# Expert stage: plain fp32 matmuls in two 64-column tiles in place of split weights

## The chip, the cores and the metric

The kernel runs on one core of a Trainium2 chip. The metric is the time of the program on the device in microseconds (us), the median of several runs. Engines are named as the profile names them: PE is TensorE's matmul and PEld its weight load, DVE is VectorE, ACT is ScalarE, POOL is GpSimd, SP is SyncE, which only issues DMAs here.

## The reference

Three layers follow each other: attention over pooled queries, a dense layer of the form `(h - tanh(h)) @ w_out`, and a routed mixture of experts. Only the last is touched:

```python
N, D, E, F = 1152, 512, 8, 1024          # tokens, model, experts, hidden
cap = N // E * 2                          # 288 rows for each expert
expert = argmax(x @ w_gate)               # one expert for each token
gate = softmax(x @ w_gate)[expert]
# tokens go to their expert in order, up to cap; later ones are dropped
h = maximum(disp[e] @ w1[e], 0)           # (cap, 512) @ (512, 1024)
y = h @ w2[e]                             # (cap, 1024) @ (1024, 512)
out[i] = gate[i] * y[expert[i], pos[i]]   # dropped tokens stay zero
```

All inputs and outputs are float32.

## The kernel before

Every step of work is an operation with candidate engines, costs and a due time (`at`). A planner, `Plan.run`, goes through them when the program is built: it takes the operation that can start earliest, finds it a place in SBUF or PSUM, and emits its instructions. Between operations marked `seq`, those of the expert stage, each engine keeps the order of their due times. DMA issues on SP are such a lane too.

The expert stage is `moe2`. Routing has sorted the tokens into a DRAM array `xs`, 288 rows for each expert, by indirect DMAs (`scatter`, L1102). The first 64 rows of each expert are handled by code that always runs; the rows 64 to 287, the overflow, by code inside `tc.If(count > 64)`, on PE, DVE and POOL. The tokens of the first two experts come from one-hot matmuls (L1181); those of the other six are loaded from `xs` (L1158) and transposed on PE (L1190). They stand in four tiles `xT`, two experts in each.

PE multiplies fp32 data in the rounded type fp32r, which keeps fewer bits. To keep accuracy each number is split: a rounded part, and what it leaves. A chunk of weights is 128 partitions x 1024 numbers, 8 for each expert (4 of `w1`, 4 of `w2`), 64 in all. `chunk` loads it by SP (L1224), copies it to the rounded type (L1235, through L421 on ACT or L423 on POOL), and subtracts (L1237, through L431 on DVE or L432 on POOL). The token tile `xT` holds the rounded part of 64 tokens and the rest side by side, 128 columns, so one matmul of 512 columns multiplies both with one part of the weights. ACT and DVE then add the two halves of the result, 64 partitions each.

For each expert `hidden` runs twice, once for each half of the 1024 hidden units (eight matmuls, L1249; the sum of halves, L1255 and L1258; four transposes, L1264; ReLU and split, L1268 and L1271), and `project` twice (eight matmuls, L1285). `output` scales by the gate, adds the halves (L1292, L1295) and scatters to the result. For an expert with overflow, `overflow_x`, `_t`, `_e`, `_h`, `_r`, `_y`, `_z` and `_s` fetch, transpose, split, multiply (L1379), apply ReLU, multiply (L1404), scale and scatter up to 224 more rows, with three products for each (rounded by rounded, and two with a rest).

The first 21 chunks (`ntot`) are requested ahead of the stage. Each later one waits until an overflow step of an earlier expert has released its place.

Of the kernel before, what the change touches and what calls it, by code (L numbers as in the profile page):

```python
# [389 lines left out]
class Kernel:  # L390
# [716 lines left out]
    def moe2(self):  # L1107
        nc, tc, P = self.nc, self.tc, self.P
        V = P.v
# [4 lines left out]
        DK, FK = DM // 128, FF // 128  # L1114
        SM = 64
        M = (cap - SM) // 2
        NP_ = 256
# [15 lines left out]
        xT = [P.sb([2, DK, 2, SM], F32R, f"xT{j}") for j in range(E // 2)]  # L1133
# [8 lines left out]
        ho = static([FK // 2, 2, 2, 2 * M], F32R, "ho")  # L1142
        xo = [static([DK, NP_], F32R, f"xo{i}") for i in range(2)]
        xbs = [static([2, 514], F32, f"xb{i}") for i in range(2)]
        yo = [static([512], F32, f"yo{i}") for i in range(2)]
        hs = P.sb([2, 512], F32, "hs")
        hT = P.sb([FK, 2 * SM], F32R, "hT")
        hp, ht, yp, ov = P.ps(2, None, "hp"), P.ps(1, None, "ht"), P.ps(1, None, "yp"), P.ps(4, None, "ov", top=True)
# [4 lines left out]
        def xe():  # L1153
            return P.raw(ho, F32).rearrange("p a b c d -> p (a b c d)")[:, 0:E // 2 * DM].rearrange("p (j d) -> p j d", d=DM)
# [9 lines left out]
        def pads():  # L1164
            for x in xo:
                nc.gpsimd.memset(V(x)[:, :, 2 * M:NP_].bitcast(F32), 0.0)

        P.op([("pool", 0.3, pads)], w=[(x, "pad") for x in xo], at=T2 - 6, name="pads")
        P.op([("dma", 2.2, lambda: ldx(1, E // 2))], r=[self.xs_tok], w=[(ho, 1)], at=T2 - 3.9, name="ldx1")
        P.op([("dma", 0.8, ldg)], r=[self.xs_tok], w=[xg], at=T2 - 3.8, name="ldg")  # L1170
        if CFG["warm"]:
            def warm():
                for i in range(CFG["warm"]):
                    nc.tensor.matmul(out=V(hp)[:, i % 2, 0:256], lhsT=self.ident_r, rhs=self.qz[0].rearrange("p a b c -> p (a b c)")[:, 0:256], start=True, stop=True)

            P.op([("pe", 0.109 * CFG["warm"], warm)], w=[hp], at=T2 - 0.6, name="warm")
# [10 lines left out]
        for j in range(E // 2):  # L1187
# [14 lines left out]
            P.op([("act", a_ps(512), lambda j=j, xpv=xpv: nc.scalar.activation(  # L1202
                out=V(xT[j])[:, :, :, 0, :], in_=xpv(), func=ACTF.Copy))], r=src, w=[(xT[j], 0)], at=at + 0.02,
                name=f"xth{j}")
            P.op([("dve", d1(512), lambda j=j, xpv=xpv: nc.vector.tensor_tensor(  # L1205
                out=V(xT[j])[:, :, :, 1, :], in0=xpv(), in1=V(xT[j])[:, :, :, 0, :].bitcast(F32), op=ALU.subtract))],
                r=src + [(xT[j], 0)], w=[(xT[j], 1)], at=at + 0.04, name=f"xtl{j}")

        def htv(half):
            return V(ht)[:, 0, half * 256:(half + 1) * 256].rearrange("p (f m) -> p f m", m=SM)  # L1210
# [3 lines left out]
        def chunk(e, q, use):  # L1214
            n = used[0]
            used[0] += 1
            wh, wl = w[e, q] = [P.sb([1024], F32R, f"{nm}{e}.{q}") for nm in ("wh", "wl")]

            def ld():
                if q < 4:  # L1220
                    src = w1[e, q % 2 * 256:(q % 2 + 1) * 256, q // 2 * 512:(q // 2 + 1) * 512]
                else:
                    src = w2[e, (q - 4) * 256:(q - 3) * 256]
                nc.sync.dma_start(out=P.raw(wl, F32).rearrange("p (k f) -> p k f", f=512),  # L1224
                                  in_=src.rearrange("(k p) f -> p k f", p=128))
# [13 lines left out]

        def hidden(e, half, at):  # L1240
            for i in range(2):
                q = 2 * half + i
                chunk(e, q, at + 0.87 * i)

                def mm(i=i, q=q):
                    for j in range(2):
                        k = 2 * i + j
                        for wl in range(2):
                            nc.tensor.matmul(out=V(hp)[:, half, :], lhsT=V(xT[e // 2])[:, e % 2, k].rearrange("p a m -> p (a m)"),  # L1249
                                             rhs=V(w[e, q][wl])[:, j * 512:j * 512 + 512],  # L1250
                                             start=(k == 0 and wl == 0), stop=(k == DK - 1 and wl == 1))

                P.op([("pe", 4 * 0.216, mm)], r=[xT[e // 2], *w[e, q]], w=[(hp, half)], at=at + 0.87 * i, name=f"h{e}.{q}")
            D = CFG["hdl"]
            P.op([("act", a_ps(512), lambda: nc.scalar.activation(  # L1255
                out=V(hs)[0:SM, half], in_=V(hp)[SM:2 * SM, half, :], func=ACTF.Copy))], r=[(hp, half)], w=[(hs, half)],
                at=at + D[0], name=f"hsc{e}.{half}")
            P.op([("dve", d1(512), lambda: nc.vector.tensor_tensor(  # L1258
                out=V(hs)[0:SM, half], in0=V(hp)[0:SM, half, :], in1=V(hs)[0:SM, half], op=ALU.add))],
                r=[(hp, half)], w=[(hs, half)], at=at + D[1], name=f"hsa{e}.{half}")  # L1260

            def trh():
                for f in range(4 * half, 4 * half + 4):
                    nc.tensor.transpose(out=V(ht)[:, 0, f * SM:(f + 1) * SM],  # L1264
                                        in_=V(hs)[0:SM, half, (f % 4) * 128:(f % 4 + 1) * 128], identity=ident[0:SM, 0:SM])
# [10 lines left out]
        def project(e, half, at):
            for i in range(2):
                f4 = 2 * half + i
                chunk(e, 4 + f4, at + 0.87 * i)
# [210 lines left out]
```

## Time and profile before

| what | value |
| --- | --- |
| median of 3 runs | 775.77 us (774.8 to 777.73) |
| the profiled execution, first to last instruction | 775.6 us |
| mean granted clock of TensorE | 0.899 of full |
| PE, DVE, ACT, POOL busy | 614.2, 626.6, 438.1, 497.8 us |
| first expert matmul / last | starts at 606.8 us / ends at 770.1 us |

The profile is of one execution and its span is within 0.2 us of the median. Busy times are of whole engines over the whole span; the expert stage is its last fifth. Matmuls are pipelined: one lasts longer than the distance between the starts of two.

### The profile page before, as it was taken

How to read it: one execution, taken by the hardware profiler on the slowest of the kernel's cores; microseconds unless marked ns; L12 is line 12 of the kernel's file. 1: busy time of each engine (PE TensorE's matmuls, PEld its weight loads, DVE VectorE, ACT ScalarE, POOL GpSimd, SP SyncE). 2: the span in 40 equal slices, each digit the busy share in tenths (PEclk: the TensorE clock that was granted, in tenths of full speed). 3: DMA queues.
4: the chain of work that ended last, by engine and by line, in shares of the span. 5: the costliest groups of instructions: out<-in, count | busy, mean ns of one | idle time of the engine just before them, and what ended most of it. 6: DMA issues, size and time to landing. Idle time of an engine off the chain costs nothing. (4 is left out here: it accounts for less than half of the span.)

```text
span 775.6 us, 9909 instructions
## 1 busy us (share of the span) xinstructions
PE 614.2 (79%) x3246; PEld 512.4 (66%) x3246; DVE 626.6 (81%) x784; ACT 438.1 (56%) x698; POOL 497.8 (64%) x359
## 2 busy tenths in 40 slices
PE   4779778788687878676877588799998698569965
PEld 3667666676576667465766477699788585449743
DVE  4998796988889989999999999774846355887483
ACT  5866766676767656655645655566633234452452
POOL 6866575785766766768669676865565516563572
PEclk9989999899999989799799897899967799779997
DMA  9899999999999997903034013233300336666520
GB/s 294 158 190 198 203 195 217 231 211 202 209 219 199 225 203 257 351 3 109 1 122 150 27 29 108 82 98 141 128 28 32 69 109 194 219 223 226 191 103 8
DMA packets 213548, 119.45 MB, mean 154 GB/s; under 512 B 172814, under 2 KB 182030, under 8 KB 213488
## 3 DMA queue, kind: packets, MB, share of 16 engines
q1 hardware_dynamic: 211600, 114.49, 60.3%
q0 software_dynamic: 1680, 3.81, 1.6%
q8 instruction: 33, 0.54, 0.3%
q10 hardware_dynamic: 208, 0.39, 0.2%
q14 instruction: 27, 0.22, 0.1%
HBM read 66.22 MB, written 11.43 MB: 100 GB/s over the span
## 5 line engine op out<-in xcount | busy, mean ns | idle before, releaser
L432 POOL TENSOR_TENSOR b<-b,b 128x512 fp32r<-128x512 f32 (+3 forms) x102 | 197.3, 1941 | 63.3 <-ACT b L421 58.3
L641 POOL TENSOR_SCALAR b<-b 128x1152 f16<-128x1152 int16 (+1 forms) x114 | 138.8, 1233 | 69.7 <-ACT b L633 37.6
L906 PE MATMUL psum<-b,b 128*128 128x512 f32 x432 | 137.4, 443 | 48.2 <-POOL b L432 26.1
L906 PEld LDWEIGHTS psum<-b,b 128*128 128x128 f32 x432 | 88.2, 212 | 71.3 <-POOL b L432 33.7
L421 ACT ACTIVATE b<-b 128x1024 fp32r<-128x1024 f32 (+3 forms) x112 | 95.1, 876 | 71.2 <-DVE b L817 21.2
L842 PE MATMUL psum<-b,b 128*128 128x384 f32 x576 | 125.5, 358 | 1.0 <-ACT b L633 0.7
L842 PEld LDWEIGHTS psum<-b,b 128*128 128x128 f32 x576 | 112.2, 204 | 9.4 <-ACT b L633 1.0
L421 ACT ACTIVATE b<-psum 64x288 f32<-64x288 f32 (+5 forms) x162 | 81.5, 508 | 61.0 <-PE psum L906 14.5
L626 DVE CUSTOM_DVE_ANT_1 b<-psum,na 128x1152 f16<-128x1152 f32 x72 | 97.2, 1350 | 16.5 <-PE psum L620 14.8
L633 ACT ACTIVATE b<-psum,b 128x1152 int32<-128x1152 f32 x72 | 87.8, 1219 | 28.1 <-DVE b L626 16.1
L431 DVE TENSOR_TENSOR b<-b,b 128x1024 fp32r<-128x1024 f32 (+1 forms) x50 | 88.5, 1774 | 16.2 <-ACT b L421 13.6
L620 PE MATMUL psum<-b,b 128*128 128x384 f32 x384 | 89.7, 373 | 14.1 <-ACT b L633 14.0
L661 PE MATMUL psum<-b,b 128*128 128x288 f16 x576 | 88.3, 300 | 4.7 <-DVE b L676 2.8
L423 POOL TENSOR_SCALAR b<-b 128x512 fp32r<-128x512 f32 (+3 forms) x48 | 52.6, 1098 | 53.2 <-DVE b L817 30.6
L620 PEld LDWEIGHTS psum<-b,b 128*128 128x128 f32 x384 | 69.8, 203 | 19.8 <-ACT b L633 19.4
L661 PEld LDWEIGHTS <-b 128*128 128x128 f16 x576 | 54.2, 102 | 24.6 <-issue 11.1
L887 POOL TENSOR_TENSOR b<-b,b 128x768 f32<-128x768 f32 x24 | 52.0, 2168 | 16.9 <-ACT b L876 15.8
L1249 PE MATMUL psum<-b,b 128*128 128x512 f32 x128 | 42.6, 487 | 7.6 <-DVE b L1205 5.9
L495 PE MATMUL psum<-ident_r,b 128*128 128x128 f32 x144 | 22.3, 274 | 21.9 <-DVE b L431 8.4
L1249 PEld LDWEIGHTS psum<-b,b 128*128 128x128 f32 x128 | 29.4, 240 | 15.2 <-DVE b L1205 6.1
L1255 ACT ACTIVATE b<-psum 64x512 f32<-64x512 f32 x16 | 9.5, 594 | 51.4 <-PE psum L1249 32.4
L817 DVE SCALAR_TENSOR_TENSOR b<-b,b 128x512 uint32<-128x512 uint32 x32 | 37.7, 1177 | 1.1
(138 smaller groups left out, 1038.4 us busy)
## 6 DMA issues: line engine op xcount, KB each, us to landing
b<-in_moe_w_dram SPq DMA_DIRECT2D x64, 512.0 KB, 5.5
b<-in_moe_w_in_dram SPq DMA_DIRECT2D x32, 256.0 KB, 4.2
b<-in_moe_w_out_dram SPq DMA_DIRECT2D x16, 512.0 KB, 5.8
xs<-b SPq DMA_DIRECT2D x6, 771.0 KB, 8.9
b<-in_k_dram SPq DMA_DIRECT2D x8, 576.0 KB, 5.3
b<-in_q_dram SPq DMA_DIRECT2D x8, 576.0 KB, 5.7
b<-in_v_dram SPq DMA_DIRECT2D x8, 576.0 KB, 4.9
out_dram<-b SPq DMA_DIRECT2D x3, 768.0 KB, 6.2
```

Of the source, the lines that this page charges most:

```text
L421: "a": ("act", (a_ps if ps else a_sb)(n), lambda: nc.scalar.activation(out=dst(), in_=src(), func=ACTF.Copy)),
L423: "p": ("pool", p1(n), lambda: nc.gpsimd.tensor_scalar(out=dst(), in0=src(), scalar1=1.0, scalar2=0.0, op0=ALU.mult, op1=ALU.add)),
L431: "v": ("dve", d1(n), lambda: nc.vector.tensor_tensor(out=dst(), in0=a(), in1=b(), op=ALU.subtract)),
L432: "p": ("pool", p2(n), lambda: nc.gpsimd.tensor_tensor(out=dst(), in0=a(), in1=b(), op=ALU.subtract)),
L620: nc.tensor.matmul(out=V(S_)[:, j, 0:CB], lhsT=lhsT, rhs=rhs[:, j * CB:(j + 1) * CB], start=(m == 0), stop=(m == len(mm) - 1))
L626: P.op([("dve", 1.27, lambda: nc.vector.tensor_tensor_reduce(out=V(junk), in0=V(S_)[:, :, 0:CB], in1=self.na[:, 3:4].unsqueeze(2).to_broad ...
L633: P.op([("act", 1.2, lambda: nc.scalar.activation(out=V(p).rearrange("p (a e) -> p a e", a=3), in_=V(S_)[:, :, 0:CB], func=ACTF.Exp, bias= ...
L641: P.op([("pool", p1(S), lambda a=a, src=src, by=by: nc.gpsimd.tensor_scalar(out=V(hl)[:, a], in0=src(), scalar1=by, scalar2=0.0, op0=ALU.m ...
L661: nc.tensor.matmul(out=V(ps)[:, 0, 0:half], lhsT=V(v16[n])[:, j].rearrange("p a d -> p (a d)"), rhs=V(pt)[:, hl * KT + j, i * SQ + g * hal ...
L842: nc.tensor.matmul(out=V(h)[:, a, 0:384], lhsT=w, rhs=V(xx)[:, dk, sl], start=(n == 0), stop=(n == 11))
L906: nc.tensor.matmul(out=V(ps)[:, 0, :], lhsT=V(g[gi, blk, i][gl])[:, a, sl], rhs=V(wo[2 * gi + i, a])[:, wl, :], start=(i == 0 and a == 0 a ...
L1249: nc.tensor.matmul(out=V(hp)[:, half, :], lhsT=V(xT[e // 2])[:, e % 2, k].rearrange("p a m -> p (a m)"), rhs=V(w[e, q][wl])[:, j * 512:j * ...
```

## The change

The rounded type leaves the expert stage. Tokens, hidden units and weights stay plain fp32 and are used as they were loaded. The 64 tokens of an expert are the stationary operand, 64 columns. Two matmuls with the same tokens and different weights write the partitions 0 to 63 and 64 to 127 of one PSUM bank, two tiles side by side. In the first layer the two tiles are the halves of the hidden units, in the second the halves of the sum over hidden units; the output adds those two, as it added the two parts before. The ReLU is done on the sums ahead of four full transposes, with one copy after. The first layer of the next expert comes ahead of the transposes of this one. 40 chunks are requested ahead and not 21. Overflow rows use plain fp32 as well: one product in place of three, on 224 columns without padding. `xT` and other buffers get fixed places.

```diff
-        xT = [P.sb([2, DK, 2, SM], F32R, f"xT{j}") for j in range(E // 2)]
+        xT = [static([2, DK, SM], F32, f"xT{j}") for j in range(E // 2)]
+        hs = [static([FH], F32, f"hs{i}") for i in range(2)]
+        hT = [static([FC, 2, SM], F32, f"hT{i}") for i in range(2)]
...
-            at = T2 - 0.5 + (0.0 if j == 0 else 3.2 + 0.2 * j)
+            at = T2 - 0.5 + (0.0 if j == 0 else 4.3 + 0.2 * j)
...
         def chunk(e, q, use):
...
-            wh, wl = w[e, q] = [P.sb([1024], F32R, f"{nm}{e}.{q}") for nm in ("wh", "wl")]
+            c = w[e, q] = P.sb([1024], F32, f"w{e}.{q}")
...
+                if q < DK:
+                    nc.sync.dma_start(out=V(c), in_=w1[e, q * 128:(q + 1) * 128, :])
...
-            P.op(self.copy_alts(lambda: V(wh), lambda: P.raw(wl, F32), 1024, CFG["ehe"][n % 8]),
-                 r=[wl, (ovt, gh)] + (latep if CFG["ehe"][n % 8] == "p" else late), w=[wh], at=at, name=f"ehi{e}.{q}")
-            P.op(self.sub_alts(lambda: V(wl), lambda: P.raw(wl, F32), lambda: V(wh).bitcast(F32), 1024, CFG["ele"][n % 8]),
...
+        def hidden(e, at):
+            h = hp[e % 2]
+            for k in range(DK):
+                chunk(e, k, at + 0.87 * k)
+
+                def mm(k=k):
+                    for i in range(2):
+                        nc.tensor.matmul(out=V(h)[i * SM:(i + 1) * SM, 0, :], lhsT=V(xT[e // 2])[:, e % 2, k],
+                                         rhs=V(w[e, k])[:, i * FH:(i + 1) * FH], start=(k == 0), stop=(k == DK - 1))
+
+                P.op([("pe", 0.87, mm)], r=[xT[e // 2], w[e, k]], w=[h], at=at + 0.87 * k, name=f"h{e}.{k}")
+            P.op([("act", a_ps(512), lambda: nc.scalar.activation(out=V(hs[e % 2]), in_=V(h)[:, 0, :], func=ACTF.Relu))],
+                 r=[h], w=[hs[e % 2]], at=at + 3.6, name=f"hs{e}")
+
+        def turn(e, at):
+            def tr():
+                for c in range(FC):
+                    nc.tensor.transpose(out=V(ht)[:, 0, c * 128:(c + 1) * 128], in_=V(hs[e % 2])[:, c * 128:(c + 1) * 128],
+                                        identity=ident)
+
+            P.op([("pe", FC * 0.11, tr)], r=[hs[e % 2]], w=[ht], at=at, name=f"ht{e}")
+            P.op([("dve", d1(512), lambda: nc.vector.tensor_copy(
+                out=V(hT[e % 2]).rearrange("p c i m -> p (c i m)"), in_=V(ht)[:, 0, :]))],
+                r=[ht], w=[hT[e % 2]], at=at + 0.1, name=f"hT{e}")
+
+        def project(e, at):
+            for c in range(FC):
+                chunk(e, DK + c, at + 0.87 * c)
+
+                def mmy(c=c):
+                    for i in range(2):
+                        nc.tensor.matmul(out=V(yp)[i * SM:(i + 1) * SM, 0, :], lhsT=V(hT[e % 2])[:, c, i],
+                                         rhs=V(w[e, DK + c])[:, i * DM:(i + 1) * DM], start=(c == 0), stop=(c == FC - 1))
...
+        for e in range(-1, E):
+            at = T2 + EP * (e + 1)
+            x0 = xbs[e % 2]
+            n = e + 1
...
+            if e >= 0:
+                over_on("t", "pe", e, at, [x0], [(ov, 0), (ov, 1)])
+                over_on("e", "dve", e, at + 0.6, [(ov, 0), (ov, 1)], [xo])
+            if n < E:
+                hidden(n, at + 0.7)
+            if e >= 0:
+                turn(e, at + 4.4)
+                over(e, 0, at + 5.0)
+                over_on("r", "dve", e, at + 5.2, [ov], [ho])
+                project(e, at + 5.6)
+                output(e, at + 9.2)
+                over(e, 1, at + 9.3)
+                over_on("z", "dve", e, at + 9.5, [(ov, 2), (ov, 3)], [x0])
+                over_on("s", "pool", e, at + 9.6, [x0, self.out_tok], [])
...
     def overflow_h(...):
-                for wl, x in ((0, xh), (0, xl), (1, xh)):
-                    for k in range(DK):
...
+                o = f % 2 * 256
+                for k in range(DK):
+                    nc.tensor.matmul(out=ps[:, f // 2, o:o + 2 * M], rhs=x[:, k, :],
+                                     lhsT=V(wsl[k])[:, f * 128:(f + 1) * 128], start=(k == 0), stop=(k == DK - 1))
     def overflow_y(...):
-                    for a, wl in ((0, 0), (0, 1), (1, 0)):
...
+                    i, c = divmod(f, FC)
+                    nc.tensor.matmul(out=ps[0:M, 2 + j, :], lhsT=V(ho)[:, f, j * M:(j + 1) * M],
+                                     rhs=V(wsl[c])[:, i * DM:(i + 1) * DM], start=(f == 0), stop=(f == FK - 1))
...
-           ... nh=16, ntot=21, ...
+           ... ntot=40, ...
```

Here `SM` is 64, `DK` 4, `FC` 4, `FH` and `DM` 512, `M` 112, `FK` 8. The second layer's loads (not shown) bring rows of both halves of `w2` into one chunk.

## Rows read from the trace of the kernel before

**Rows 1.** The page's table of engines: busy us, share, instructions.
```profile
PE 614.2 (79%) x3246; PEld 512.4 (66%) x3246; DVE 626.6 (81%) x784; ACT 438.1 (56%) x698; POOL 497.8 (64%) x359
```
**Rows 2.** Windows: length, busy PE, PEld, DVE, ACT, POOL, PE clock, DMA share, GB/s.
```profile
620.10:632.00 11.90, 11.90 (x99) 11.84 (x98) 4.83 (x9) 1.44 (x2) 0.00 (x0) 1.00 0.00 1
...
662.00:679.00 17.00, 11.53 (x44) 7.97 (x44) 14.58 (x11) 9.45 (x13) 10.51 (x5) 0.80 0.75 250
...
606.70:775.60 168.90, 133.69 (x636) 103.55 (x636) 108.17 (x104) 66.60 (x88) 80.96 (x42) 0.87 0.47 153
```
**Rows 3.** Groups by form, 600 to 776 us: busy us, mean ns, idle before.
```profile
L431 DVE TENSOR_TENSOR b<-b,b 128x1024 fp32r<-128x1024 f32 x34 | 70.2, 2067 | 4.5 <-ACT b L421 2.0 <-DVEq L1412 1.1 <-DVEq L1387 1.1
L432 POOL TENSOR_TENSOR b<-b,b 128x1024 fp32r<-128x1024 f32 x22 | 59.2, 2698 | 40.3 <-ACT b L421 39.3 <-issue 0.2
L421 ACT ACTIVATE b<-b 128x1024 fp32r<-128x1024 f32 x45 | 45.5, 1049 | 11.1 <-PE psum L1404 6.0 <-PE psum L1379 4.9
...
L1379 PEld LDWEIGHTS psum<-b,b 128*128 128x128 f32 x192 | 23.2, 192 | 0.2
...
L1205 DVE TENSOR_TENSOR b<-psum,b 128x512 fp32r<-128x512 f32 x4 | 2.8, 691 | 6.5 <-ACT b L1202 6.4
```
**Rows 4.** Timelines of one ordinary expert, DVE and PE: start, us, what, idle before.
```profile
735.07 2.08 PE L1249 MATMUL psum<-b,b 128*128 128x512 f32 x8
...
737.86 3.08 DVE L431 TENSOR_TENSOR b<-b,b 128x1024 fp32r<-128x1024 f32 x1
...
741.18 3.04 DVE L431 TENSOR_TENSOR b<-b,b 128x1024 fp32r<-128x1024 f32 x1 [0.24 <-DVEq L1387]
744.14 0.67 DVE L1258 TENSOR_TENSOR b<-psum,b 64x512 f32<-64x512 f32 x1
...
744.87 0.69 PE L1264 MATMUL psum<-ident,b 64*128 64x64 f32 x4 [4.76 <-DVE b L1258]
745.70 3.28 PE L1249 MATMUL psum<-b,b 128*128 128x512 f32 x8
749.28 2.08 PE L1285 MATMUL psum<-b,b 128*128 128x512 f32 x8 [0.30 <-PEq L1350]
```
**Rows 5.** Timeline of SP's queue, 430 to 640 us: its loads of expert weights.
```profile
451.53 106.54 SPq L1224 DMA_DIRECT2D b<-in_moe_w_dram  x21
...
631.31 1.92 SPq L1224 DMA_DIRECT2D b<-in_moe_w_dram  x4
```
**Rows 6.** Timeline of PE, 578 to 650 us.
```profile
595.01 5.85 PE L1181 MATMUL psum<-b,b 128*128 128x128 f32 x50
...
611.55 2.82 PE L1190 MATMUL psum<-ident,b 128*128 128x128 f32 x12 [0.98 <-DMA b<-xs]
...
620.12 11.88 PE L1379 MATMUL psum<-b,b 128*128 128x256 f32 x96
...
635.97 11.40 PE L1404 MATMUL psum<-b,b 128*112 128x512 f32 x48
```
**Rows 7.** Timelines of DVE, POOL, SP's queue and ACT, 578 to 612 us.
```profile
581.87 2.03 DVE L1071 TENSOR_TENSOR b<-b,b 128x24 f32<-128x24 f32 x1
583.93 0.18 DVE L1072 TENSOR_TENSOR b<-b,b 128x24 f32<-128x24 f32 x1
...
596.68 4.61 DVE L431 TENSOR_TENSOR b<-b,b 128x1024 fp32r<-128x1024 f32 x4
...
597.72 4.43 POOL L1102 DMA_INDIRECT xs<-b,xi  x1 [0.30 <-issue]
602.46 0.97 POOL L1102 DMA_INDIRECT xs<-b,xi  x1 [0.30 <-issue]
...
604.75 0.69 SPq L1158 DMA_DIRECT2D b<-xs  x1
...
605.41 0.60 ACT L1202 ACTIVATE b<-psum 128x512 fp32r<-128x512 f32 x1 [9.11 <-DMA xs<-b,xi]
```
**Rows 8.** Timeline of PE: the last matmuls.
```profile
767.95 2.12 PE L1285 MATMUL psum<-b,b 128*128 128x512 f32 x8 [0.93 <-DVEq L1387]
```

More of the change, by code (lines that the diff above doesn't have):

```diff
@@ L1114, in moe2 @@
         DK, FK = DM // 128, FF // 128
+        FH = FF // 2
+        FC = FK // 2
         SM = 64
         M = (cap - SM) // 2
-        NP_ = 256
         T2 = self.t2 + CFG["t2"]
@@ L1141, in moe2 @@
         xg = P.sb([E, 2], F32, "xg")
-        ho = static([FK // 2, 2, 2, 2 * M], F32R, "ho")
-        xo = [static([DK, NP_], F32R, f"xo{i}") for i in range(2)]
+        ho = static([FK, 256], F32, "ho")
+        xo = static([DK, 2 * M], F32, "xo")
         xbs = [static([2, 514], F32, f"xb{i}") for i in range(2)]
[L1145 to L1148, printed above, removed]
+        xT = [static([2, DK, SM], F32, f"xT{j}") for j in range(E // 2)]
+        hs = [static([FH], F32, f"hs{i}") for i in range(2)]
+        hT = [static([FC, 2, SM], F32, f"hT{i}") for i in range(2)]
+        yo = [P.sb([512], F32, f"yo{i}") for i in range(2)]
+        for y in yo:
+            y.limit = P.limit
+        hp = [P.ps(1, None, f"hp{i}") for i in range(2)]
+        ht, yp, ov = P.ps(1, None, "ht"), P.ps(1, None, "yp"), P.ps(4, None, "ov", top=True)
         xv = xs.rearrange("(e s) d -> s e d", s=cap)
@@ L1201, in moe2 @@
                 P.op([("pe", DK * 0.11, trx)], r=[(ho, 1)], w=[(ov, j)], at=at, name=f"xtr{j}")
[L1202 to L1210, printed above, removed]
+            eng = "av"[j % 2]
+            P.op(self.copy_alts(lambda j=j: V(xT[j]), xpv, 512, eng, True), r=src, w=[xT[j]], at=at + 0.02, name=f"xth{j}")
         rel, w, used = {}, {}, [0]
@@ L1240, in hidden @@
[L1240 to L1265, printed above, removed]
-            P.op([("pe", 4 * 0.11, trh)], r=[(hs, half)], w=[(ht, half)], at=at + D[2], name=f"htr{e}.{half}")
-            P.op([("act", a_ps(256), lambda: nc.scalar.activation(
-                out=V(hT)[:, 4 * half:4 * half + 4, 0:SM], in_=htv(half), func=ACTF.Relu))],
-                r=[(ht, half)], w=[(hT, half)], at=at + D[3], name=f"hth{e}.{half}")
-            P.op([("dve", d1(256), lambda: nc.vector.scalar_tensor_tensor(
-                out=V(hT)[:, 4 * half:4 * half + 4, SM:2 * SM], in0=htv(half), scalar=0.0,
-                in1=V(hT)[:, 4 * half:4 * half + 4, 0:SM].bitcast(F32), op0=ALU.max, op1=ALU.subtract))],
-                r=[(ht, half)], w=[(hT, half)], at=at + D[4], name=f"htl{e}.{half}")
@@ L1276, in project @@
[L1276 to L1279, printed above, removed]
-                def mmy(f4=f4):
-                    for f in range(2 * f4, 2 * f4 + 2):
-                        for wl in range(2):
-                            o = (f % 2) * DM
-                            nc.tensor.matmul(out=V(yp)[:, 0, :], lhsT=V(hT)[:, f, :], rhs=V(w[e, 4 + f4][wl])[:, o:o + DM],
-                                             start=(f == 0 and wl == 0), stop=(f == FK - 1 and wl == 1))
-                P.op([("pe", 4 * 0.216, mmy)], r=[(hT, half), *w[e, 4 + f4]], w=[yp], at=at + 0.87 * i, name=f"y{e}.{f4}")
+                if q < DK:
+                    nc.sync.dma_start(out=V(c), in_=w1[e, q * 128:(q + 1) * 128, :])
+                else:
+                    nc.sync.dma_start(out=V(c).rearrange("p (i f) -> p i f", i=2),
+                                      in_=w2[e].rearrange("(i c p) d -> c p i d", i=2, p=128)[q - DK])
@@ L1398, in overflow_y @@
         FK = FF // 128
+        FC = FK // 2
         ps = V(ps4)
@@ L1402, in overflow_y, with overflow_z @@
                 for f in range(FK):
[L1403 to L1408 removed]
+                    i, c = divmod(f, FC)
+                    nc.tensor.matmul(out=ps[0:M, 2 + j, :], lhsT=V(ho)[:, f, j * M:(j + 1) * M],
+                                     rhs=V(wsl[c])[:, i * DM:(i + 1) * DM], start=(f == 0), stop=(f == FK - 1))
+    def overflow_z(self, reg, xb, xo, ho, ps4, SM, M):
         nc, tc, V = self.nc, self.tc, self.P.v
```

118 lines of the change are left out of this document (32 added, 86 removed).

## The prediction

> **What bounds the kernel now.** I read the page's table of engines first. It names no bound: TensorE is busy for 79% of the span, VectorE for 81% [rows 1]. Those are averages over stages, so next come the windows of the stage that the change touches, from the first matmul of the experts (606.7 us) to the end: 168.9 us, in which PE is busy for 133.7, DVE for 108.2 and POOL for 81.0, at a granted clock of 0.87 [rows 2]. Two kinds of stretch hide in that sum. While an overflowing expert runs its extra matmuls (620.1 to 632), PE has no gap and the clock is 1.00. From 662 to 679 us, one ordinary expert, PE is busy for 11.5 of 17.0 us, DVE for 14.6, and the clock is 0.80. Only two of the eight experts overflow; so six are bound by something that is not PE.
>
> The groups of instructions of the stage say what: splitting the weights. L431 takes 70.2 us of DVE, L432 59.2 of POOL, L421 45.5 of ACT [rows 3]. The timeline of one ordinary expert shows how that reaches PE [rows 4]: two subtractions of 3.08 and 3.04 us stand on DVE ahead of the addition L1258, and the transposes L1264 wait 4.76 us for it. The price is paid twice: behind the gap eight matmuls take 3.28 us where eight took 2.08 ahead of it, and with a mean granted clock of 0.80 part of such an expert ran at 1.2 and not at 2.4 GHz.
>
> Loading doesn't limit the stage: 21 chunks were requested by 558 us, and the queue then requested none until 631 us, for want of buffers [rows 5].
>
> **The splits go.** 64 copies and 64 subtractions leave ACT, DVE and POOL, 175 us of the stage in the three groups above. What an ordinary expert leaves to DVE is a copy of 128x512 from PSUM (0.69 us, priced as L1205 [rows 3]) and the multiply-add of the output; to POOL, the scatter. So the gaps of 4.8 us and the slow clock behind them go, and what is late next is PE itself.
>
> **The price of plain fp32.** The trace has such matmuls, the one-hot products L1181: 36 in the code, 72 in the trace, so one fp32 matmul is two instructions. Fifty instructions of 128 columns take 5.85 us, 0.117 each [rows 6]. The rounded type takes 11.88/96 = 0.124 us for 256 columns (L1379) and 11.40/48 = 0.238 for 512 (L1404): 0.00044 us a column and 0.010 fixed. An fp32 column thus costs as much as two rounded ones, and 512 of them 4 x (0.117-0.010) + 0.010 = 0.44 us. One layer of one expert (4 row chunks, 2 tiles, 2 instructions) is 16 of these, 7.0 us one after another. Today it is two groups of eight at 2.08 us, 4.2 us.
>
> **Side by side.** Nothing in this trace runs two 64-column tiles at once, so I bound the layer from both sides: 7.0 us if they run in turn, half of it if all overlaps. Program order makes it worse than half: tile A's two instructions, then tile B's two, and the second of A must follow the first on the same columns. If matmuls start in order, A's second overlaps B's first, and B's second the next first of A: 9 slots of 0.44 = 3.9 us. Weight loads mostly hide: L1379's loads of 128 columns take 0.192 us, yet its matmuls come every 0.124 us [rows 3, 6]. A load of 64 columns is 0.10 us, an estimate, half of that row's. Each change of tile may expose one: 7 x 0.10 = 0.7. I take 4.7 us a layer, between 3.9 (nothing exposed) and 5.3 (7 x 0.19). I choose the overlapping side because the two tiles share neither array columns nor output partitions.
>
> The Trainium skill (TensorE: Matmul & The Clock Gate, Measured speedup vs the span model) has a price for this, 2.38 times for three column tiles; the same share of the ideal would be 1.59 times for two, an estimate from that page: 4.4 us a layer, and a sum some 5 us below mine. No row here shows it.
>
> **Overflow.** First layer: 32 matmuls of 224 columns, 64 instructions of 0.20 us (0.107 x 224/128 + 0.010; by the rounded rows 448 x 0.00044 + 0.010 = 0.21): 12.8 us against 11.88. Second: 32 instructions of 0.44, 14.1 against 11.40. PE has no gap there today, so both add to the path: 3.6 us for each of two experts.
>
> **The order.** Each iteration now runs the next expert's first layer ahead of this one's transposes, so the ReLU on ACT (0.6 us, as L1202 [rows 7]) lies under it. What stays open is transposes, copy, second layer: 4 transposes at a third of L1190's 2.82 us, halved since those ran behind a gap, 0.46 [rows 6]; the copy 0.69; handover to PE 0.06 (L1258 ends at 744.81, L1264 starts at 744.87 [rows 4]) and a last transpose's drain, which I put at 0.17. Branches on PE cost 0.30 once where nothing covers them, as ahead of L1285 [rows 4]. An ordinary expert: 4.7 + 0.46 + 0.92 + 4.7 + 0.3 = 11.1 us. An overflowing one, whose extra matmuls cover the copy and whose extra transposes are 8 of that kind: 0.9 + 4.7 + 0.46 + 12.8 + 4.7 + 14.1 + 0.5 = 38.2.
>
> **The start.** Splits also stand in the routing chain. L1071, on 128x24, takes 2.03 us beside a POOL subtraction, where the same form just after takes 0.18; the second scatter takes 4.43 us where the third takes 0.97, while four L431 run on DVE [rows 7]. Without these the last scatter's issue, now over at 603.4, is over some 3 + 3.4 us earlier, near 597, and its rows have landed by 598.5. The first expert's tokens come from L1181, not from the scatter; still, ACT's copy of them now waits 9.11 us for the scatter, by my reading because its buffer lies over the one scattered from. The fixed place frees it, and the first expert's first layer fits ahead of 604. PE's next work, the transposes of tokens from DRAM, needs the load L1158: issued at 604.75 today, transposes at 611.55, 6.8 us. On SP it now stands behind forty chunk loads and not 21, and the last of them can start only as the tokens' buffer comes free, at that same scatter. Bounds: 598.5 + 6.8 = 605.3 with nothing ahead; with eight chunks ahead, of 0.52 MB at 250/0.75 = 333 GB/s [rows 2], 1.6 us each, 13 us later, 618. I take one or two chunks: 607.5, 4 us earlier than today.
>
> **Later loads.** 24 chunks are left. Each four are requested behind an overflow step, the first four behind the first expert's, and are needed some three experts later. At 1.6 us they take 38 us in all, spread over 100: hidden. If not, PE would wait in the fifth expert.
>
> **The sum.** Transposes from 607.5, 2.8 long: 610.3. First expert 38.2, and 1.2 for a slow clock behind the wait (3.28-2.08): 649.7. Three ordinary ones: 683.0. The fifth overflows: 721.2. Two ordinary: 743.4. The last has no first layer ahead, 6.4: 749.8. From the last matmul to the end, 775.6 - 770.1 = 5.5 [rows 8]: **755.3 us** against the profiled span of 775.6. The median of the runs, 775.77, is 0.2 away, so the forecast is 755 us.
>
> **Rivals.** (1) The tiles run in turn. For it: no two matmuls at once in the trace, and an fp32 matmul is already two instructions. Price: 16 layers x (7.0-4.7) = +37, **792 us**, slower. Break-even is a layer of 4.7 + 20.3/16 = 6.0 us: it decides where running side by side saves less than 1.0 of the 7.0 us.
>
> (2) Weight loads don't hide beside a matmul in the other tile: nothing overlaps then, 16 x (0.44+0.10) = 8.6 us a layer, +62, **817 us**. Against it: L1379's loads overlap running matmuls that use the same rows [rows 3, 6]. The Trainium skill (TensorE: Matmul & The Clock Gate, The mechanism) says that weight loads overlap running matmuls only where the row groups differ; two column tiles share all rows, so by that rule this is the case. The trace disagrees for the undivided array, and shows nothing for tiles.
>
> (3) The tokens' load comes behind the chunks: transposes at 613 to 618, +6 to +11, **761 to 766 us**. For it: SP's order. Against it: the buffers of the stage before come free one by one, and 21 loads were out 50 us early.
>
> **Chances.** Forecast 0.68, its own range 742 to 767 (16 x 0.8 below, 16 x 0.6 above, 2 for the start); late start 0.12; in turn 0.16; exposed loads 0.04. The range leaves out the last two: 739 to 775, its top a late start with a slow layer. About 0.5%, 4 us, can be told from no change: faster 0.76, same 0.04, slower 0.20.
>
> **What would show it.** Right: no split of weights on DVE or POOL; instructions of a layer starting 0.29 us apart on average; ordinary experts 11 us apart; PE idle for about 1 us ahead of a second layer; a clock near 1.00 from 615 us on. Wrong: layers near 7 us (rival 1); loads that start only as a matmul ends (2); the first transposes after 613 us with PE idle ahead of them (3); PE waiting for a chunk in the fifth expert; or a stage of routing that ends no earlier, its splits gone.

## The result, and the profile after

The changed kernel takes **754.33 us** (749.81 to 756.94), against 775.28 for the kernel before in the same rounds: 0.9725 of its time, 95% interval 0.9686 to 0.9763. The forecast was 755 us. The profiled execution took 752.86 us, its span is 751.1. The median came out within a microsecond of the forecast; several of the terms did not, and their errors cancel. The forecast was a sum up to the end of the span, 755.3 us, and the span measured is 4.2 us less.

The page's table of engines, answering to [rows 1], and windows of five stretches, answering to [rows 2]:

```profile
PE 602.6 (80%) x3118; PEld 470.4 (63%) x3118; DVE 532.2 (71%) x705; ACT 372.0 (50%) x617; POOL 412.3 (55%) x325
```

```profile
598.00:606.40 8.40, 0.87 (x5) 0.00 (x0) 0.00 (x0) 0.00 (x0) 0.76 (x1) 0.82 0.98 272
606.40:613.90 7.50, 0.00 (x0) 0.03 (x1) 0.00 (x0) 0.00 (x0) 0.00 (x0) 0.50 0.82 240
613.90:751.10 137.20, 119.13 (x492) 61.54 (x492) 23.21 (x34) 10.73 (x17) 11.83 (x13) 0.96 0.32 107
652.00:684.00 32.00, 24.95 (x115) 9.78 (x116) 4.79 (x8) 3.84 (x6) 4.42 (x5) 0.97 1.01 351
684.44:690.16 5.72, 5.72 (x18) 1.54 (x17) 0.62 (x1) 0.00 (x0) 0.00 (x0) 0.62 0.20 71
```

DVE and POOL have all but left the expert stage: from the token transposes to the end, DVE is busy for 23 of 137 us, and PE for 119, at a granted clock of 0.96. Ahead of it lie 15 us in which PE does nothing but wait, while the DMA engines are busy at 0.98 and 0.82.

The groups of the stage by form (606 to 751.1 us) hold no split, in place of [rows 3]:

```profile
L1247 PE MATMUL psum<-b,b 128*64 128x512 f32 x128 | 29.2, 597 | 5.9 <-DVEq L1342 5.9
L1357 PE MATMUL psum<-b,b 128*112 128x512 f32 x64 | 28.0, 595 | 0.0
L1223 PE MATMUL psum<-b,b 128*64 128x512 f32 x112 | 27.8, 641 | 2.8 <-PEq L1311 2.8
L1336 PE MATMUL psum<-b,b 128*128 128x224 f32 x128 | 24.5, 352 | 0.0
```

L1247 and L1357 last the same, 597 and 595 ns. Yet 128 of L1247 take 29.2 us where 64 of L1357, which use the array undivided, take 28.0: the tiles of L1247 overlap in pairs. PE's timeline, answering to [rows 4, 6, 8] (a row is a run of instructions of one kind: start, duration, what, idle before it):

```profile
595.22 3.65 PE L1223 MATMUL psum<-b,b 128*64 128x512 f32 x16 [1.58 <-ACT b L421]
613.90 2.79 PE L1183 MATMUL psum<-ident,b 128*128 128x128 f32 x12 [15.04 <-DMA b<-xs]
...
621.73 12.27 PE L1336 MATMUL psum<-b,b 128*128 128x224 f32 x64
...
637.51 13.99 PE L1357 MATMUL psum<-b,b 128*112 128x512 f32 x32
...
661.48 3.65 PE L1223 MATMUL psum<-b,b 128*64 128x512 f32 x16 [0.57 <-PEq L1311]
665.06 0.66 PE L1233 MATMUL psum<-ident,b 128*128 128x128 f32 x4
666.59 3.65 PE L1247 MATMUL psum<-b,b 128*64 128x512 f32 x16 [0.88 <-DVEq L1342]
670.82 3.65 PE L1223 MATMUL psum<-b,b 128*64 128x512 f32 x16 [0.57 <-PEq L1311]
...
682.79 1.72 PE L1315 MATMUL psum<-ident,b 112*128 112x112 f32 x8 [3.20 <-DMA b<-xs]
684.44 5.79 PE L1223 MATMUL psum<-b,b 128*64 128x512 f32 x16
...
741.90 3.65 PE L1247 MATMUL psum<-b,b 128*64 128x512 f32 x16 [1.63 <-DVEq L1342]
```

A layer is 3.65 us, and one ordinary expert is 9.34 us from the next (661.48 to 670.82). The transposes of tokens start at 613.90 and not at 607.5. And there is a wait that nobody had on the list: at 682.79 PE waits 3.20 us for the fifth expert's overflow rows, and the layer behind that wait takes 5.79 us, at a mean granted clock of 0.62 (last of the windows).

How a layer comes to 3.65 us is seen in the weight loads of one second layer (timeline of PEld) and in the view of its line:

```profile
657.71 0.17 PEld L1247 LDWEIGHTS psum<-b,b 128*64 128x64 f32 x2 [0.26 <-issue]
658.14 0.17 PEld L1247 LDWEIGHTS psum<-b,b 128*64 128x64 f32 x2 [0.26 <-issue]
```

```profile
L1247 PEld LDWEIGHTS psum<-b,b x16: 133/137/137, 657.2 to 659.9; 128*64 128x64 f32 x16
L1247 PE MATMUL psum<-b,b x16: 592/592/643, 657.3 to 660.3; 128*64 128x512 f32 x16
```

Two loads go out every 0.43 us, the pace of one 512-column instruction (the forecast had 0.44), while two matmuls of 0.59 us each are in flight. The loads of 0.137 us add nothing to that pace.

The chain of work that ended last shows the late start (start, duration, what), in place of [rows 7]:

```profile
592.21 5.74 DMA xs<-b,xi
597.97 8.07 DMA b<-xs
606.06 0.33 SPq L1207
606.43 0.69 SPq L1162
607.12 0.05 issue
607.23 6.70 DMA b<-xs
```

The last scatter is issued 10.25 us earlier than before (592.21 against 602.46 [rows 7]). ACT's half of the token load goes out at 597.97 and lands 8.07 us later. SP's half stands behind the fortieth chunk load L1207, which itself went out only at 606.06; it goes out at 606.43 and lands 7.3 us later, at 613.8. (The chain's last row is the small load of the gates, issued right behind it.) Of 10.25 us won, the first transposes keep none: 613.90 against 611.55 [rows 6].

Two more delays are in these rows. The scatter itself took 5.74 us from issue to landing; it takes 2.26 with 21 chunks ahead (594.56 to 596.82). And the fortieth chunk load was not slow to start, it waited for ACT's half (SP's waits, 585 to 615 us: who waited, for what, us in total, times, longest):

```profile
SPq L1207 <- DMA b<-xs: 5.4, 1, 5.4
```

In the trace the loads of SP and ACT signal eight semaphores in turn, and each goes out only when the load before it on its semaphore has landed. The fortieth chunk comes eight loads behind ACT's half. So the two halves of the tokens, meant to go side by side, went one after the other.

The fifth expert's overflow rows are requested by POOL at 673.87 and land 8.8 us later; PE had finished its work before them at 679.6:

```profile
673.87 0.73 POOL L1305 DMA_DIRECT2D b<-xs  x1 [0.94 <-PE psum L1223]
```

### The profile page after: what moved, and what is told of

Its sections match the earlier page's. It is cut to its first block, busy times and chain, and to the rows that moved or that the text cites. A ratio compares the mean times of both kernels' runs of the same rounds, so it can differ in the third digit from the quotient of the medians.

```text
span 751.1 us, 9324 instructions
## 1 busy us (share of the span) xinstructions
PE 602.6 (80%) x3118; PEld 470.4 (63%) x3118; DVE 532.2 (71%) x705; ACT 372.0 (50%) x617; POOL 412.3 (55%) x325
## 5 line engine op out<-in xcount | busy, mean ns | idle before, releaser
L906 PE MATMUL psum<-b,b 128*128 128x512 f32 x432 | 140.0, 450 | 46.0 <-POOL b L432 24.9
L432 POOL TENSOR_TENSOR b<-b,b 128x512 fp32r<-128x512 f32 (+2 forms) x78 | 132.2, 1702 | 25.0 <-ACT b L421 19.7
L906 PEld LDWEIGHTS psum<-b,b 128*128 128x128 f32 x432 | 89.6, 216 | 69.4 <-POOL b L432 32.0
L842 PEld LDWEIGHTS psum<-b,b 128*128 128x128 f32 x576 | 111.8, 203 | 9.1 <-ACT b L633 1.2
L661 PE MATMUL psum<-b,b 128*128 128x288 f16 x576 | 90.2, 304 | 3.2 <-ACT b L421 1.9
L620 PEld LDWEIGHTS psum<-b,b 128*128 128x128 f32 x384 | 70.8, 205 | 20.6 <-ACT b L633 20.0
L423 POOL TENSOR_SCALAR b<-b 128x512 fp32r<-128x512 f32 (+2 forms) x40 | 43.0, 1079 | 56.9 <-DVE b L817 30.0
L1102 POOL DMA_INDIRECT out_dram<-b,b x8 | 7.3, 915 | 113.8 <-DVE b L1257 66.4
L421 ACT ACTIVATE b<-b 128x576 fp32r<-128x576 f32 (+2 forms) x56 | 38.7, 703 | 52.4 <-DVE b L817 20.1
L880 DVE SCALAR_TENSOR_TENSOR b<-b,b 128x768 f32<-128x768 f32 x24 | 37.8, 1575 | 2.1 <-ACT b L859 1.6
L817 DVE SCALAR_TENSOR_TENSOR b<-b,b 128x512 uint32<-128x512 uint32 x32 | 37.6, 1177 | 1.1
L815 DVE SCALAR_TENSOR_TENSOR b<-b,b 128x512 uint32<-128x512 uint32 x32 | 37.8, 1180 | 0.2
L892 DVE COPY_PREDICATED b<-b,b 128x768 f32<-128x768 uint32 x24 | 30.8, 1281 | 8.3 <-POOL b L887 7.8
```

Source lines behind the costliest of these rows:

```text
L421: "a": ("act", (a_ps if ps else a_sb)(n), lambda: nc.scalar.activation(out=dst(), in_=src(), func=ACTF.Copy)),
L423: "p": ("pool", p1(n), lambda: nc.gpsimd.tensor_scalar(out=dst(), in0=src(), scalar1=1.0, scalar2=0.0, op0=ALU.mult, op1=ALU.add)),
L432: "p": ("pool", p2(n), lambda: nc.gpsimd.tensor_tensor(out=dst(), in0=a(), in1=b(), op=ALU.subtract)),
L620: nc.tensor.matmul(out=V(S_)[:, j, 0:CB], lhsT=lhsT, rhs=rhs[:, j * CB:(j + 1) * CB], start=(m == 0), stop=(m == len(mm) - 1))
L661: nc.tensor.matmul(out=V(ps)[:, 0, 0:half], lhsT=V(v16[n])[:, j].rearrange("p a d -> p (a d)"), rhs=V(pt)[:, hl * KT + j, i * SQ + g * hal ...
L815: nc.vector.scalar_tensor_tensor(out=V(t), in0=lo(), scalar=29, in1=V(t), op0=ALU.logical_shift_right, op1=ALU.bitwise_or)
```

## The experiments

All ratios are against the kernel before, run on the same chip. Unless a sentence says otherwise the edit is to the changed kernel.

**One tile for both halves.** The second tile is given up: both halves use columns 0 to 63, with the same number of matmuls. Not shown: the first layer's halves go to two PSUM banks, so the ReLU is two instructions on ACT, and the output, with nothing left to add, is one on DVE.

```diff
-    nc.tensor.matmul(out=V(h)[i * SM:(i + 1) * SM, 0, :], ...
+    nc.tensor.matmul(out=V(hp[i])[0:SM, 0, :], ...
...
-    nc.tensor.matmul(out=V(yp)[i * SM:(i + 1) * SM, 0, :], ... start=(c == 0), stop=(c == FC - 1))
+    nc.tensor.matmul(out=V(yp)[0:SM, 0, :], ... start=(c == 0 and i == 0), stop=(c == FC - 1 and i == 1))
```

> Plain fp32, nothing split, but no two tiles: both halves of each layer go through the same 64 columns of the array, the first layer's into two PSUM banks, the second layer's summed in one. Theory (running side by side pays; a layer of 3.65 us in the changed kernel becomes 16 x 0.43 + 0.16 = 7.0): 16 layers x 3.4 = +54 us, about 808 us, slower than the kernel before. Rival (dropping the splits is what pays and PE has slack): within 5 us of the changed kernel's 754.

Measured 800.48 us, 1.0304 (1.0262 to 1.0346). Two layers in PE's timeline:

```profile
660.80 7.05 PE L1222 MATMUL psum<-b,b 128*64 128x512 f32 x16 [0.65 <-PEq L1309]
...
669.22 7.08 PE L1248 MATMUL psum<-b,b 128*64 128x512 f32 x16 [0.78 <-DVEq L1340]
```

The same instructions take 7.05 to 7.08 us in one tile and 3.65 in two, a factor of 1.93. Without the second tile, dropping the splits for plain fp32 makes the kernel slower. Fifteen layers lie behind the first transposes: 15 x 3.4 = 51 us, less the 5.3 us of the fifth expert's wait, which is not there (0.43 us idle at that place), gives 754.3 + 51 - 5.3 = 800 us. (The transposes started 1.9 us later in this execution, which is not in the sum.)

**Tile after tile.** All eight instructions of a layer for the first tile are issued ahead of the eight for the second.

```diff
-            for k in range(DK):
...
-                def mm(k=k):
-                    for i in range(2):
+            def mm(i):
+                for k in range(DK):
...
+            P.op([("pe", 4 * 0.87, lambda: (mm(0), mm(1)))], ...
```

> The two tiles stay in their own columns, but each layer issues all eight instructions of the first tile ahead of all eight of the second. Theory (matmuls start in program order, so only the last of one tile meets the first of the other): layers near 6.6 us, 16 x 2.9 = +47, about 800 us. Rival (the engine looks far enough ahead to start the second tile by itself): no change, 754 us.

Measured 778.08 us, 1.0017 (0.9997 to 1.0037): the whole gain is gone. A layer takes 5.39 to 5.42 us, which neither side had said (6.6 and 3.65):

```profile
666.69 5.39 PE L1248 MATMUL psum<-b,b 128*64 128x512 f32 x16 [0.88 <-DVEq L1344]
```

Fifteen layers of 1.75 us more, a start 3.1 us later (616.99) and 5.3 us less for the fifth expert's wait, which is not there, give 778 us. The timeline of PEld in one first layer:

```profile
660.29 0.14 PEld L1223 LDWEIGHTS psum<-b,b 128*64 128x64 f32 x1 [0.29 <-issue]
...
661.58 0.19 PEld L1223 LDWEIGHTS psum<-b,b 128*64 128x64 f32 x3 [0.29 <-issue]
662.00 0.19 PEld L1223 LDWEIGHTS psum<-b,b 128*64 128x64 f32 x2 [0.24 <-issue]
...
662.92 0.14 PEld L1223 LDWEIGHTS psum<-b,b 128*64 128x64 f32 x1 [0.29 <-issue]
```

One load for each 0.43 us for four slots, then two or three, then one again for the last four: twelve slots and a part, 5.39 us. The second tile's first matmul thus starts about when the first tile's fifth does, ahead of three earlier ones that still wait for their turn in the first tile. By this reading PE does start a matmul ahead of earlier ones of another tile, some three ahead and no more. Which record belongs to which tile is inferred from the steps of 0.43 us, since the trace doesn't name the tile; that the starts don't keep program order is shown by the 5.39 us, as in order they would need fifteen slots, 6.6 us. In the changed kernel two instructions of one tile alternate with two of the other, which is within that reach; so all its slots are filled.

**Tokens on ACT's queue.** Both halves of the token load are issued by ACT, past SP's forty chunk loads.

```diff
-            for i, q in enumerate((nc.sync, nc.scalar)):
-                q.dma_start(
+            for i in range(2):
+                nc.scalar.dma_start(
```

> Both halves of the load of tokens are issued from ACT's queue, none behind the chunks on SP. Theory (the 15 us that PE waits ahead of the token transposes are SP's order: the second half is issued at 606.4 us, 8.5 us behind the first): both issued by 598.7, transposes near 606, 8 us less, about 746 us. Rival (the DMA engines are full with chunk loads, share 0.98 there, and set the landing whoever issues): transposes after 611, at most 3 us less.

Measured 754.19 us, 0.9706 (0.9671 to 0.9740), the time of the changed kernel. ACT's and PE's timelines:

```profile
599.96 1.33 ACTq L1162 DMA_DIRECT2D b<-xs  x2
```

```profile
613.40 2.79 PE L1183 MATMUL psum<-ident,b 128*128 128x128 f32 x12 [12.58 <-DMA b<-in_moe_w_dram]
```

The two issues are over by 601.3 us, where SP's half went out at 606.43; yet the transposes start only 0.5 us earlier. The releaser named is a chunk load whose semaphore the transposes also read; the tokens themselves were as late. SP's second load of the gates, on the same semaphore as the tokens' second half, waits for that half until 613.28 (SP's waits):

```profile
SPq L1166 <- DMA b<-xs: 4.0, 1, 4.0
```

The halves were issued at 599.96 and 600.67, and landed 7.7 and 12.6 us later. So SP's order alone was not what kept the tokens away; chunk loads were in flight beside them. This run leaves open how much the second half lost by following the first on one queue.

**21 chunks ahead.** `ntot=40` becomes `ntot=21`, the number of before.

> 21 chunks requested ahead, as before the change, and not 40; all else as changed. Theory (the preload is not needed, and what it does is to push the load of tokens back): transposes near 605, the later chunks land in time as each four are requested some 20 us ahead of their use, about 746 us. Rival (43 chunks of 1.5 us don't keep up with ordinary experts of 9.3 us and 8 chunks each): PE waits for weights in the second to fourth expert, 5 to 15 us, about 755 to 765 us.

Measured 744.78 us, 0.9576 (0.9527 to 0.9626). SP's queue and PE:

```profile
596.87 0.69 SPq L1162 DMA_DIRECT2D b<-xs  x1
```

```profile
607.02 1.53 PE L1183 MATMUL psum<-ident,b 128*128 128x128 f32 x12 [3.46 <-DMA b<-xs]
...
674.04 1.73 PE L1315 MATMUL psum<-ident,b 112*128 112x112 f32 x8 [3.00 <-DMA b<-xs]
675.69 4.39 PE L1223 MATMUL psum<-b,b 128*64 128x512 f32 x16
```

The start comes 6.9 us earlier and PE never waits for a chunk. Up to the transposes PE, DVE, ACT and POOL run the same instructions in the same order as with 40, so it is the loads and not another plan. The nineteen more chunks ahead cost 9.5 us and bought nothing. The fifth expert's wait stays, and the layer behind it is slow.

**40 ahead, tokens first.** The count stays; the token load is issued ahead of the last chunk loads. By SP's queue 21 of them go out before it and 19 behind it, not 20 and 20 as expected.

```diff
-    P.op([("dma", 2.2, lambda: ldx(1, E // 2))], ... at=T2 - 3.9, name="ldx1")
+    P.op([("dma", 2.2, lambda: ldx(1, E // 2))], ... at=T2 - CFG["eld"] + 2.05, name="ldx1")
```

> 40 chunks are still requested ahead of any release by an overflow step, but SP's half of the token load stands behind 20 chunk loads, ahead of the other 20. Theory: the landing of the tokens is set by the chunk loads in flight with them, not by how many chunks have a place; so the token transposes start near 607 us as with 21 ahead, and the time is 745 us (742 to 748). Rival: the 20 loads issued right behind the token load share the DMA engines with it all the same; transposes then start at 611 to 614 us, and the time is 751 to 754 us.

Measured 744.39 us, 0.9598 (0.9563 to 0.9634), the time with 21 ahead.

```profile
594.26 0.69 SPq L1162 DMA_DIRECT2D b<-xs  x1
```

```profile
603.59 2.82 PE L1183 MATMUL psum<-ident,b 128*128 128x128 f32 x12 [2.65 <-DMA b<-xs]
```

The start is earlier than the 607 us expected, as in this execution the last scatter went out at 591.94, and at 594.56 with 21 ahead. Forty places do no harm; chunk loads that are in flight when the tokens come do. ACT's half shows it best, as nothing stands ahead of it in its queue. It went out at 594.22, and PE's sequencer passed its wait for it at 598.9 (view of the line):

```profile
L1183 PEldq EVENT_SEMAPHORE  x1: 51/51/51, 598.9 to 598.9; - x1
```

That is 4.7 us, as with 21 ahead (596.84 to 601.6) and in the kernel before (604.63 to 609.4); in the changed kernel it was 8.07. The last scatter lands in 2.26 us again. Chunk loads issued right behind SP's half cost less: 9.3 us from issue to transposes here and 10.2 with 21 ahead, against 6.8 in the kernel before [rows 6, 7]. So three things made the late start: a scatter that landed late, an ACT half that landed late, and SP's half that had to wait for both.

**Overflow transposes later, 21 and 40 ahead.** The overflow transposes of an expert, and DVE's copies of them, are issued behind the next expert's first layer.

```diff
-                over_on("t", "pe", e, at, [x0], [(ov, 0), (ov, 1)])
-                over_on("e", "dve", e, at + 0.6, [(ov, 0), (ov, 1)], [xo])
+                over_on("t", "pe", e, at + 3.5, [x0], [(ov, 0), (ov, 1)])
+                over_on("e", "dve", e, at + 3.6, [(ov, 0), (ov, 1)], [xo])
```

> 21 chunks ahead, as in the run before (744.8 us), and the overflow transposes of an expert (and the copies behind them) issued after the next expert's first layer and not ahead of it. Theory: the rows of the fifth expert landed 3.0 us after PE wanted them and within the 3.65 us that a first layer takes, so the wait goes and with it the slow clock behind it (4.39 in place of 3.65 us): 744.8 - 3.0 - 0.7 = 741 us. Rival: the transposes and two copies now lie open between first layer and overflow, and DVE does those copies ahead of the copy that PE waits for, about 1.4 us for each of two overflowing experts; the gain then goes to 743.9.

> The changed kernel with 40 chunks ahead and with nothing altered but the place of the overflow transposes, behind the next expert's first layer. Theory: the fifth expert's wait (3.2 us) and the slow layer behind it (5.79 in place of 3.65) go, 5.3 us; and the branch that stood open at 0.57 us ahead of the first layer of each ordinary expert shrinks, 0.27 us for each of five experts, 1.4 us: 754.3 - 6.7 = 747.6 us, and the start stays at 613 to 614 us. Rival: only the branch's part is kept, since the rows land too late for the transposes' new place as well: 751 to 753 us.

Measured 737.15 us with 21 ahead, 0.9509 (0.9478 to 0.9540), and 748.91 us with 40, 0.9659 (0.9592 to 0.9726). PE's timeline with 21 ahead:

```profile
649.32 3.65 PE L1223 MATMUL psum<-b,b 128*64 128x512 f32 x16
...
658.38 3.65 PE L1223 MATMUL psum<-b,b 128*64 128x512 f32 x16 [0.15 <-PEq L1353]
...
667.45 3.65 PE L1223 MATMUL psum<-b,b 128*64 128x512 f32 x16 [0.15 <-PEq L1353]
671.03 0.98 PE L1315 MATMUL psum<-ident,b 112*128 112x112 f32 x8
```

The wait is gone, and the layer ahead of the transposes takes 3.65 us. The open branch of 0.57 us went down to 0.15, so an ordinary expert takes 9.07 us in place of 9.34. The theory for 40 (747.6) lies within the interval, which is wide and overlaps that of the changed kernel. With 21 the gain is 7.6 us and not 3.8. The two profiled executions lie further apart, 10.5 us: 3.0 + 0.7 are the wait and the slow clock, some 1.2 the branches (five times 0.23, as ordinary experts were 9.30 us apart with 21), 1.7 a slow last layer (5.33 us in the run before, 3.65 here), and 3.0 an earlier start (604.07 against 607.02 us). For the last two the edit gives no reason that I have shown. With 40 the start came 2.6 us later than in the changed kernel (616.47), with the same work ahead of it, so executions differ by that much.

**The order undone.** On top of the kernel with 21 ahead and later transposes, the next expert's first layer is issued behind this one's second.

```diff
-            if n < E:
+            if n == 0:
                 hidden(n, at + 0.7)
...
+                if n < E:
+                    hidden(n, at + 9.7)
```

> As the kernel with the later overflow transposes, but the first layer of the next expert is issued after this one's second layer, so that nothing stands on PE between a first layer and the transposes of its result. Theory: the order hides the ReLU (0.6 us) and two handovers; for each of seven experts the transposes wait 0.8 to 0.9 us more: +6 us, 747 us if the other kernel is at 741. Rival: the longer gap also lets TensorE's clock fall behind it (an ordinary expert has then two gaps of 0.9 us in 9 us): a layer at the lower clock takes up to 5.4 us, +10 to +20 us, 751 to 761 us. Third possibility: under 2 us, if PE's branches cover the ReLU.

Measured 740.18 us, 0.9532 (0.9507 to 0.9558), 3.0 us above the other order. The intervals overlap, so the times alone don't show a difference; the trace shows where one would come from.

```profile
654.50 0.66 PE L1233 MATMUL psum<-ident,b 128*128 128x128 f32 x4 [0.75 <-ACT b L1227]
...
659.75 3.65 PE L1223 MATMUL psum<-b,b 128*64 128x512 f32 x16 [0.16 <-PEq L1355]
```

The transposes now wait 0.75 us for the ReLU, where a branch had stood open for 0.16: 0.59 us at each of six places, 3.5 us. The theory's 6 us forgot the branch and counted the overflowing experts, where the other transposes fill the gap. The clock does not fall: layers stay at 3.65 us.

**16 and 12 ahead.** Also on top of the later transposes.

> As the kernel with the later overflow transposes, with 16 chunks requested ahead and not 21. Theory: at 21 the token load was issued within a few us of the last scatter and took about as long as before the change, so the chunk loads no longer set its landing: the same time, 741 us within 2. Rival: five loads fewer still bring the tokens earlier, transposes at 605 and 739 us. Other rival: the third expert's chunks, now requested only after the first expert's overflow step, are late: PE waits for them near 650 us, and the time is above 744.

> As the kernel with 16 chunks ahead (730.5 us) and with the later overflow transposes, but 12. Theory: loading then sets the pace. Every group of four chunks is released one overflow step later: the four of the third expert's first layer behind the first expert's second overflow step, near 638 us, which is when PE wants them; four loads took 4 us or more from the first issue, so PE waits 5 us there and, with 8 chunks of 0.52 MB for each ordinary expert of 9.07 us (462 GB/s, where 382 was the most that was seen), again in each ordinary expert, 2 to 4 us each: 745 us or more, slower than with 16. Rival: the loads come fast enough, and fewer chunks free the routing stage further: 730 or less.

With 16: **730.49 us**, 0.9402 (0.9375 to 0.9428), the best version of this study. With 12: 735.33 us, 0.9474 (0.9415 to 0.9534). With 16 the transposes start at 599.00 us, 5 us earlier than with 21. This comes from further up. Windows from 560 to 578 us, first with 21, then with 16 ahead:

```profile
560.00:578.00 18.00, 15.06 (x57) 12.72 (x55) 7.09 (x17) 3.44 (x8) 6.70 (x5) 0.62 0.12 44
```

```profile
560.00:578.00 18.00, 17.18 (x108) 14.63 (x107) 9.68 (x26) 5.08 (x11) 11.71 (x9) 1.00 0.14 54
```

With 16 PE does 108 instructions in these 18 us, at the full clock, where it did 57 at 0.62, and the last scatter is issued at 586.93 us in place of 593.44. With fewer chunks the planner lays out the stage before in another order (PE's instructions part from the other plan at 552 us). That order was not tried by itself, so the 6.7 us are a fact of this plan and not a rule about loads. The intervals with 16 and 12 overlap. With 12, loading does reach PE, but once, and for less than I had said:

```profile
664.17 1.08 PE L1223 MATMUL psum<-b,b 128*64 128x512 f32 x4 [1.80 <-DMA b<-in_moe_w_dram]
665.60 4.46 PE L1223 MATMUL psum<-b,b 128*64 128x512 f32 x12 [0.35 <-DMA b<-in_moe_w_dram]
```

This is at the end of the three ordinary experts, as the prediction had it for loads that are not hidden. The theory placed it 26 us earlier: it took the overflow step that releases a chunk for something that SP waits for, but SP issued twelve chunks from 616.70 to 624.85 us, eight of which the theory had put behind 638.

## Why the prediction was right, and where it was not

Against the profiled span, 755.3 forecast and 751.1 measured, by the prediction's own sum (the transposes' end is where PE's next work starts):

| step | forecast | measured | difference |
| --- | --- | --- | --- |
| token transposes end | 610.3 | 616.5 | +6.2 |
| first expert, overflowing | 39.4 | 35.0 | -4.4 |
| three ordinary experts | 33.3 | 28.1 | -5.2 |
| fifth expert, overflowing | 38.2 | 40.9 | +2.7 |
| two ordinary experts | 22.2 | 18.6 | -3.6 |
| last expert | 6.4 | 6.5 | +0.1 |
| tail | 5.5 | 5.5 | 0.0 |

That the median was met within 0.7 us is luck, twice over. Errors of up to 6.2 us cancel in the sum. And the prediction took the span for the time of the program, since the one profile lay 0.2 us from the median; in every run on record the time is 1.7 to 1.8 us above the span, and this profiled execution was 1.5 us faster than the median.

**What bounds the stage** was right. With the splits gone PE sets the pace, with 0.9 us open at the copy (0.92 forecast, 0.88 measured at 666.59) and a clock of 0.96.

**The price of plain fp32** was right: 0.43 us for an instruction of 512 columns, 7.05 us for 16 in one tile (forecast 0.44 and 7.0). The overflow layers, 12.27 and 13.99 us, were forecast at 12.8 and 14.1.

**Side by side** was right in kind and too dear in size: 4.7 us against 3.65, below the lower bound of 3.9. Two assumptions failed. Starts in order would cost a ninth slot; 3.65 us hold eight, and the run of tile after tile doesn't fit starts in order either. And no weight load is exposed at a change of tile. Fifteen layers behind the start: -16 us.

Rival 2 falls: loads of 0.137 us that use all rows go out while two matmuls run, and a pair still comes every 0.43 us. The Trainium skill (TensorE: Matmul & The Clock Gate, The mechanism) says that loads overlap running matmuls only in other row groups; the trace disagrees. The same section of the Trainium skill says that matmuls start and end strictly in order; the twelve slots of the tile-after-tile run do not fit strict starts. The Trainium skill (TensorEngine Tiling (Array Packing), Key Properties) says that different tiles load and multiply in parallel; the trace agrees, with 1.93 times for two tiles. The prediction's estimate from the Trainium skill (TensorE: Matmul & The Clock Gate, Measured speedup vs the span model), 4.4 us, was nearer than its sum and still too high.

**The start** was wrong: rival 3 came true, at 0.12, with the sign given for it (transposes after 613 us, PE idle ahead of them). The part on routing more than held (the last scatter's issue was over at 593.2 us and not near 597). What comes behind it did not. I allowed 1.5 us for its rows to land, and they took 4.8 (593.2 to 597.95). I took one or two chunk loads ahead of the tokens; the DMA engines were full when ACT's half went out, and SP's half waited for that half. The rival had SP's order right and not the wait for ACT's half behind it. +6.2 us, as that rival priced it; it did not come to 761 us because the layers were quicker.

**Later chunk loads** never made PE wait, as said. But the prediction looked only at the chunks: the fifth expert's overflow rows, which POOL requests, travel with the same burst (351 GB/s from 652 to 684 us). Their load took 8.8 us; it took 7.6 in the kernel before and 7.5 in the run of one tile, where PE didn't wait. What is new is above all that the quicker experts leave 5.7 us between request and need, where those two left some 17 and 14. That wait of 3.2 us and the slow layer behind it, 2.1, were in no step and no rival. Moving the transposes behind the next first layer removes them.

**The order** was right in kind: the ReLU is hidden. By the waits it is worth about 3 us; the times, with overlapping intervals, don't confirm it.

## What to carry to other kernels

Two 64-column tiles nearly double plain fp32 (7.05 to 3.65 us a layer), but only if their instructions alternate closely; issued tile after tile they give back half of that (5.39). More loads ahead are not safer: a load that the next step waits for should find the DMA engines empty, so issue it ahead of loads that are needed later, and look at every small load that falls into a burst. A forecast that meets the time is no proof of its steps; here five of seven terms were off by 2.7 to 6.2 us, and their sum by 4.2.

## What was not expected of the hardware

- PE starts a matmul of one tile ahead of earlier ones of the other, some three deep by the reading above: a layer issued tile after tile takes 5.39 us, and in order it would take 6.6.
- 64-column weight loads of fp32 (0.137 us) add nothing beside matmuls in both tiles: 16 matmuls in 3.65 us, a pair every 0.43.
- A layer that ran mostly at 1.2 GHz took up to 5.8 us in place of 3.65 in the changed kernel, and the length of the gap ahead does not tell which one does. The first layer behind 15.04 us of idle (at 617.65) took 3.65 us at a clock of 1.00, the one behind 3.20 us took 5.79 at 0.62. Between gap and layer PE did transposes, 3.75 us of them at 0.57 in the first case and 1.65 at 0.50 in the second: in the first the clock was back before the layer began.
